# FNet mixing plus MLP on one core: the work around the paired blocks in another order

## The chip, the cores and the metric

The kernel runs on one NeuronCore of a Trainium2 chip. The metric is the device time of one execution, in microseconds (us). Three executions of the kernel before took 879.98, 880.30 and 880.65 us.

## The reference

The input x has 2048 rows and 640 columns. After a layer norm it goes through two branches, whose results are added to x. All inputs and the output are float32.

```python
xn = (x - mean) / sqrt(var + 1e-5)                       # over the 640 columns
a, b = xn @ wr.T, xn @ wi.T                              # DFT along the columns, wr and wi 640 x 640
A = cr @ a - ci @ b                                      # DFT along the rows, real part, cr and ci 2048 x 2048
B = gelu(xn @ w1 + b1) @ w2 + b2                         # w1 640 x 1536, w2 1536 x 640
out = x + A + B
```

## The kernel before

Every operand of a matmul is split in two, a high half that ScalarE rounds to fp32r (`high`, line 182) and a low half that VectorE gets by subtraction (`low`, line 185); `product` (lines 303 to 305) then takes three matmuls: high x high, high x low, low x high. Each reads 128 x 128 weights against 512 columns. The order of all instructions is written out by hand: every engine runs its own list in the order in which the code issues it, and waits where its data or its place is not ready. A tile of a pool with one buffer can be written only when every reader of the tile that lay there before is done, stores to memory included. Loads and stores go through the queue of SyncE (SP), in that same order: a load or store that waits holds up all behind it.

The 2048 rows are four row blocks t = 0 to 3 of 512, and the 1536 hidden units are 12 chunks of 128. The kernel runs in these stages:

- **Block 0, a loop over i = 0 to 9.** Step i splits W1 of chunk i + 3 (`prep_w1`) and W2 of chunk i + 1 (`prep_w2`), issues two weight loads, calls `background(i)`, and then does `hidden(i + 2)` (15 matmuls, line 321), its gelu and split (the tile `hs`), and `output(i)` (15 matmuls). `background` normalizes the rows of blocks 2 and 1 (`ln_stats`, `ln_scale`, `ln_apply`), stores them to the DRAM buffer xs, and loads them back, turned, as Z["b"] (block 2, tile z_b) and Z["a"] (block 1, tile row). `make_forms` turns parts of Z with VectorE and splits them; each is a *form* (ua, va, oa from "a"; vb, ob, t1 from "b"; t2, t3, t4 from sums and differences of both).
- **Six paired blocks, k = 0 to 5.** `pair(k)` does the first MLP layer of blocks 1 and 2 for two hidden chunks at once, by a scheme in which 7 products take the place of 8 (Strassen's, in Winograd's form). `window` multiplies a *piece* of the weights (A, B, C, D, each split in a high half "h" and a low half "l" by `make_pieces`, with "+" for the sums between) with a form. The gelu of block 1 stays on chip (a1, a2), that of block 2 goes to the DRAM buffer gs (`keep`). `put_out` places output matmuls of block 1 between the windows. `beside_pair(k, at)` holds other work, and is called in a block in the order at = 2, 5, 6, 3, 7, 4: finishing block 0 (`finish`: ScalarE adds the bias, VectorE turns the block, GpSimd adds it to x in xo[0]), storing it (`store_sums`), copying rows in DRAM (`by_chunks`), and splitting the seven forms of the column DFT matrices wr and wi (`prep_w`, `put_w`), which are stored to the buffers wits.
- **A loop over p = 0 to 13.** Step p does `output` of block 2 from the stored units, or, at the end, block 3's first hidden chunks. `between(p)` holds the rest: finishing block 1, layer norm of the last rows (x12 to x15), Z["z"] for block 3, splitting W1 again, loading xo[2].
- **Block 3, and from 290 us on the DFT along the rows**, in which TensorE's work is matmul after matmul.

In `put_w` before, five of the forms share three places of the tile wst in turn, and two lie in the pool rows under the tag "yt":

```python
        if w in (3, 4):
            t = rows.tile([P, 2, 2 * P], F32R, tag="yt", bufs=2, name=f"wst{w}_{j}")
        else:
            t = A["wst"][:, A["puts"] % 3]
```

Names that the prediction uses: "Al" is the low half of piece A; C2 is the window (z_, "C", 2, "vb") of a block, t4 the window (x_, b, 0, "t4"); zc is ScalarE's copy of the bank z_ that must be made before C2 overwrites it; b2 is the second unit of block 2 in a paired block. The tiles wst, xo[0], z_b and others lie in turn in the one place of the pool outp (`zo_tile`).

Of the kernel before, what the change touches and what calls it, by code (L numbers as in the profile page):

```python
# [15 lines left out]
P = 128  # L16
# [9 lines left out]
def kernel(  # L26
# [198 lines left out]
    def ln_apply(c, eng=nc.vector):  # L225
        m = MV[:, slot[c]]
        eng.tensor_scalar(xt[c], xt[c], m[:, 0:1], m[:, 3:4], op0=ALU.subtract, op1=ALU.mult)
        nc.sync.dma_start(xs[c * P : (c + 1) * P], xt[c])
# [146 lines left out]
    def add_block(dst, e, acc, name, eng=nc.gpsimd, bias=None, home=rows):  # L375

        if bias is not None:
            nc.scalar.activation(acc, acc, AF.Identity, bias=bias)
        yt = home.tile([P, TB], F32, tag="yt", bufs=2, name=name)
        nc.vector.transpose(yt, acc)  # L380
        d = dst[:, :, e * B : (e + 1) * B]
        eng.tensor_tensor(d, d, yt.rearrange("p (n i) -> p n i", i=B), op=ALU.add)  # L382
# [21 lines left out]
    stores = []  # L404

    def put_away():
        for f in stores:
            f()
        stores.clear()

    def put_w(w, j, main, odd=None, negative=False):

        n = GWIDE[w] * P
        if w in (3, 4):
            t = rows.tile([P, 2, 2 * P], F32R, tag="yt", bufs=2, name=f"wst{w}_{j}")
        else:
            t = A["wst"][:, A["puts"] % 3]
            A["puts"] += 1
        split(t[:, 0, : 2 * P], t[:, 1, : 2 * P], main)
        if odd is not None and not negative:  # L420
            split(t[:, 0, 2 * P :], t[:, 1, 2 * P :], odd)
        elif odd is not None:
            h, l = t[:, 0, 2 * P :], t[:, 1, 2 * P :]
            nc.scalar.activation(h, odd, AF.Copy, scale=-1.0)
            nc.vector.scalar_tensor_tensor(l, odd, -1.0, h.bitcast(F32), op0=ALU.mult, op1=ALU.subtract)
        stores.append(lambda: nc.sync.dma_start(wits[w][j], t[:, :, :n].bitcast(F32)))

    def prep_w(j, k):
# [20 lines left out]
        put_away()  # L449
# [252 lines left out]
    def background(i):  # L702

        if i == 0:
            ln_apply(0)
            ln_apply(1)
            A["rows_b"] = zo_tile("rows_b", (P, NC, D))
            for c in range(2 * NC, 3 * NC):
                load_x(c, home=A["rows_b"])
        if i == 1:  # L710
            ln_apply(2)
            ln_apply(3)
            for c in range(NC, 2 * NC):
                load_x(c)
        if i == 2:
            for c in range(2 * NC, 3 * NC):
                ln_stats(c)
        if i == 3:
# [3 lines left out]
            ln_stats(4)  # L722
            ln_stats(5)
            Z["b"] = zo_tile("z_b")
            load_z(Z["b"], 2)
        if i == 4:
            ln_stats(6)
            ln_stats(7)
# [4 lines left out]
            load_z(Z["a"], 1)  # L733
        if i == 6:
            new_forms()
            make_forms("b", "vb0", "vb1", "ob0")
        if i == 7:
            make_forms("a", "ua0", "ua1", "va0", "va1", "oa0")
        if i >= 8:
            (ua, va), (ub, vb) = ((Z[k][:, :, : 2 * B], Z[k][:, :, 2 * B : 4 * B]) for k in "ab")  # L740
        if i == 8:
            add(ub, ub, ua, ALU.subtract)
            make_forms("b", "t10", "t11")
            add(vb, vb, ub, ALU.subtract)
        if i == 9:
            add(ua, vb, ua, ALU.subtract)
            add(va, va, vb, ALU.subtract)
            turn_x("t20", "b")
            turn_x("t21", "b")
# [6 lines left out]
    def new_forms():  # L756
        spare = []
        for k, name in enumerate(("ua", "va", "t1", "vb")):
# [4 lines left out]
        XF["oa0"], XF["ob0"] = spare[:2], spare[2:]  # L763
# [73 lines left out]
    def finish(t, *es):  # L837
        for e in es:
            add_block(xo[t], e, oacc[t][e], f"ot{t}_{e}", bias=b2c[:, e : e + 1])
# [5 lines left out]
    def store_sums(t):  # L845
        for k, (c0, c1) in enumerate(YCOLS):
            nc.sync.dma_start(ys[k][t], xo[t][:, :, c0:c1])  # L847

    LASTK = NF // 2 - 1

    def beside_pair(k, at):

        if k == 0:
# [6 lines left out]
            if at == 7:  # L860
                finish(0, 0, 1, 2)
            if at == 4:
                finish(0, 3, 4)
            return
        j = k - 1
        if at == 2 and k > 1:
            prep_w(j - 1, 2)
        if at == 5:
            if k > 1:
                put_away()  # L870
            else:
                store_sums(0)
            if k < NT:
                by_chunks(k - 1)
        if at == 6:
            turn_w(0, j)
            turn_w(1, j)
        if at == 3:
            if k == 1:
                A["wst"], A["puts"] = zo_tile("wst", (P, 3, 2, 3 * P), F32R), 0  # L880
# [4 lines left out]
            put_away()  # L885
# [3 lines left out]
        if at == 7:  # L889
# [6 lines left out]
            put_away()  # L896
# [3 lines left out]
        if k == LASTK and at == 4:  # L900
# [703 lines left out]
```

## Time and profile before

| | us |
|---|---|
| three runs | 879.98, 880.30, 880.65 (median 880.3) |
| profiled execution | 878.27 |
| its span, first to last instruction | 876.3 |
| TensorE (PE) busy | 852.8 |
| VectorE (DVE) busy | 683.4 |
| ScalarE (ACT) busy | 364.8 |
| GpSimd (POOL) busy | 22.1 |
| mean DMA rate over the span | 201 GB/s |

In the profile's lines a time is us from the span's start. A line of a timeline gives start, length, engine, line of the kernel, operation, tiles (out<-in), shapes and count, and in brackets the idle time of the engine before it and what ended that. "SPq" is SyncE's queue at the moment of issue. A line of the waits gives who waited for whom: us in total, how often, the longest. A line of the windows gives a stretch, its length, and each engine's busy time and instructions in it, then the clock granted to TensorE, the busy share of the DMA engines, and GB/s.

### The profile page before, as it was taken

What the parts mean: (1) busy time and instruction counts of PE and PEld (TensorE: products, weight loads), DVE (VectorE), ACT (ScalarE), POOL (GpSimd) and SP (SyncE); (2) the same over time, 40 slices, a digit from 0 to 9 for tenths busy, and PEclk for the clock granted to TensorE, in tenths of its full rate; (3) what the DMA queues carried; (4) which work ended last, traced back from release to release, by engine and by line L of the source; (5) the groups of instructions that cost most, each with busy time, mean ns of one, the idle gap of its engine ahead of it and who ended that gap; (6) DMA issues with size and microseconds to landing.
All of it is one profiled execution on the core that took longest, in us unless ns stands there. A gap on an engine that the chain in (4) does not pass through costs nothing.

```text
span 876.3 us, 10521 instructions
## 1 busy us (share of the span) xinstructions
PE 852.8 (97%) x3718; PEld 700.2 (80%) x3718; DVE 683.4 (78%) x892; ACT 364.8 (42%) x520; POOL 22.1 (3%) x22
## 2 busy tenths in 40 slices
PE   8999889999989999999999999999999999999996
PEld 6888667788867888888888888888888888888885
DVE  6787887675773478988988798898977898885586
ACT  5564456455534356543433434332322423223241
POOL 0000030000111100000000000000000000000000
PEclk9999899999999999999999999999999999999999
DMA  6987488879987993968583459855575779804464
GB/s 182 301 239 165 94 200 270 261 225 302 277 229 158 223 422 159 215 143 196 155 216 85 99 145 321 232 104 154 142 179 190 235 192 229 317 18 174 120 186 84
DMA packets 227187, 171.76 MB, mean 196 GB/s; under 512 B 83648, under 2 KB 197056, under 8 KB 226496
## 3 DMA queue, kind: packets, MB, share of 16 engines
q1 hardware_dynamic: 221184, 169.13, 70.5%
q10 hardware_dynamic: 5952, 1.97, 0.9%
q8 instruction: 29, 0.48, 0.2%
q14 instruction: 22, 0.18, 0.1%
HBM read 124.92 MB, written 51.38 MB: 201 GB/s over the span
## 4 chain that ended last, share of the span: by engine, by line
PE 67%; DMA 4%; SPq 2%; DVE 1%; POOL 1%; issue 0%; ACT 0%; POOLq 0%; DVEq 0%; ACTq 0%
PE banks L303 21%; PE banks L304 21%; PE banks L305 21%; PE banks L321 3%; DMA xab<-in_A_x_dram 1%; DMA w1r<-in_B_w_dram 1%; DMA xo<-in_A_x_dram 1%; SPq L281 1%; DMA wit<-wst 1%; POOL xo L382 0%; SPq L847 0%; SPq L373 0%; DMA xs<-row 0%; SPq L258 0%; DVE as L185 0%
## 5 line engine op out<-in xcount | busy, mean ns | idle before, releaser
L304 PE MATMUL banks<-as,xab 128*128 128x512 f32 x407 | 158.4, 389 | 0.0
L303 PE MATMUL banks<-as,xab 128*128 128x512 f32 x407 | 158.4, 389 | 0.0
L305 PE MATMUL banks<-as,xab 128*128 128x512 f32 x407 | 158.4, 389 | 0.0
L182 ACT ACTIVATE as<-r 128x1024 fp32r<-128x1024 f32 x80 | 85.0, 1062 | 173.6 <-PE banks L305 148.8
L185 DVE TENSOR_TENSOR as<-r,as 128x1024 fp32r<-128x1024 f32 x80 | 97.2, 1216 | 39.1 <-ACT as L182 39.1
L304 PEld LDWEIGHTS banks<-as,xab 128*128 128x128 f32 x407 | 76.4, 188 | 16.2 <-DVE as L185 0.4
L305 PEld LDWEIGHTS banks<-as,xab 128*128 128x128 f32 x407 | 76.4, 188 | 15.9
L303 PEld LDWEIGHTS banks<-as,xab 128*128 128x128 f32 x407 | 76.4, 188 | 15.9
L303 PE MATMUL banks<-as,xc 128*128 128x512 f32 x224 | 87.1, 389 | 0.0
L304 PE MATMUL banks<-as,xc 128*128 128x512 f32 x224 | 87.1, 389 | 0.0
L305 PE MATMUL banks<-as,xc 128*128 128x512 f32 x224 | 87.1, 389 | 0.0
L182 ACT ACTIVATE as<-rt 128x1024 fp32r<-128x1024 f32 x32 | 34.0, 1063 | 69.8 <-PE banks L305 57.9
L321 PE MATMUL banks<-xt,xab 128*128 128x512 f32 x240 | 56.8, 390 | 0.3 <-ACT xt L182 0.3
L185 DVE TENSOR_TENSOR hs<-ab,hs 128x512 fp32r<-128x512 f32 x36 | 26.7, 743 | 36.2 <-ACT hs L182 36.2
L321 PEld LDWEIGHTS banks<-xt,xab 128*128 128x128 f32 x240 | 44.7, 188 | 10.3 <-ACT xt L182 1.3
L305 PEld LDWEIGHTS banks<-as,xc 128*128 128x128 f32 x224 | 42.0, 188 | 8.8
L303 PE MATMUL banks<-hs,xc 128*128 128x512 f32 x120 | 47.0, 392 | 2.1 <-DVE ot L380 2.1
L303 PEld LDWEIGHTS banks<-as,xc 128*128 128x128 f32 x224 | 42.0, 188 | 8.7
L304 PEld LDWEIGHTS banks<-as,xc 128*128 128x128 f32 x224 | 42.0, 188 | 8.7
L305 PE MATMUL banks<-hs,xc 128*128 128x512 f32 x120 | 46.7, 389 | 0.0
L304 PE MATMUL banks<-hs,xc 128*128 128x512 f32 x120 | 46.7, 389 | 0.0
L185 DVE TENSOR_TENSOR as<-rt,as 128x1024 fp32r<-128x1024 f32 x32 | 38.8, 1212 | 5.3 <-ACT as L182 5.3
(200 smaller groups left out, 1601.7 us busy)
## 6 DMA issues: line engine op xcount, KB each, us to landing
raw<-in_A_dft_seq_re_dram SPq DMA_DIRECT2D x64, 256.0 KB, 5.3
raw<-in_A_dft_seq_im_dram SPq DMA_DIRECT2D x64, 256.0 KB, 4.9
w1r<-in_B_w_dram SPq DMA_DIRECT2D x136, 80.0 KB, 2.7
wit<-wst SPq DMA_DIRECT2D x20, 384.0 KB, 3.1
ws<-wit SPq DMA_DIRECT2D x15, 384.0 KB, 5.5
xn<-xs SPq DMA_DIRECT2D x4, 1280.0 KB, 7.8
forms_ab<-xab SPq DMA_DIRECT2D x4, 1280.0 KB, 8.1
xab<-wit SPq DMA_DIRECT2D x13, 384.0 KB, 4.4
```

The source lines that it names most:

```text
L182: nc.scalar.activation(h, s, AF.Copy)
L185: nc.vector.tensor_tensor(l, s, h.bitcast(F32), op=ALU.subtract)
L281: eng.dma_start(t[q * B : (q + 1) * B], v[q, :, :, f0 : f0 + P])
L303: nc.tensor.matmul(acc, wh, mh, start=first, stop=False, skip_group_check=goes_on)
L304: nc.tensor.matmul(acc, wh, ml, start=False, stop=False, skip_group_check=goes_on)
L305: nc.tensor.matmul(acc, wl, mh, start=False, stop=last, skip_group_check=goes_on)
L321: nc.tensor.matmul(acc, W1[i][:, a, j * P : (j + 1) * P], XT[j][:, b], start=n == 0, stop=n == len(steps) - 1)
```

## The change

It moves work among the steps above, and puts some tiles elsewhere; the arithmetic stays.

- **background**: all four `ln_apply` of block 0's rows in step 0, their stores behind the loads of the next rows (`put_rows`); the statistics of blocks 2 and 1 one step sooner; the forms from "b" in step 5, from "a" in steps 6 and 7; the sums and differences one step sooner, the turns of t2 ahead of those of step 9.
- **new_forms**: the forms lie in the four places in another order, and the fourth place is opened a step later.
- **make_pieces** in steps of another order (D ahead of C, the B piece of block 0 after the loop); in block k = 0 the pieces D and C for the next block come after the gelu of a2.
- **finish of block 0**: blocks 0 and 1 after the gelu of a2 in k = 0 (`at == 4`), block 2 at `at == 2` and blocks 3 and 4 at `at == 5` of k = 1; some turned blocks lie in the pool mr under the tag "zt".
- **put_out**: 3 and 3 output groups where there were 2 and 4.
- **put_w**: a place of its own for each form, form 2 in two parts (one store more); the last three forms at the end of their own block (`at == 4`) and not in the next.
- **LASTK (k = 5) and between**: load_unit(6, 7) ahead of x14 and x15; statistics of the last rows in p = 0 to 2, `ln_apply` in p = 2; the turns of Z["z"] in p = 7 to 9; load_xo(2) in p = 9; finish of blocks 1 and 2 spread over other steps and places.

```diff
-    def ln_apply(c, eng=nc.vector):
+    def ln_apply(c, eng=nc.vector, put=True):
         m = MV[:, slot[c]]
         eng.tensor_scalar(xt[c], xt[c], m[:, 0:1], m[:, 3:4], op0=ALU.subtract, op1=ALU.mult)
+        if put:
+            put_rows(c)
+    def put_rows(c):
         nc.sync.dma_start(xs[c * P : (c + 1) * P], xt[c])
...
-    def add_block(dst, e, acc, name, eng=nc.gpsimd, bias=None, home=rows):
+    def add_block(dst, e, acc, name, eng=nc.gpsimd, bias=None, home=rows, tag="yt"):
...
             nc.scalar.activation(acc, acc, AF.Identity, bias=bias)
-        yt = home.tile([P, TB], F32, tag="yt", bufs=2, name=name)
+        yt = home.tile([P, TB], F32, tag=tag, bufs=2, name=name)
         nc.vector.transpose(yt, acc)
...
-    stores = []
-    def put_away():
-        for f in stores:
-            f()
-        stores.clear()
     def put_w(w, j, main, odd=None, negative=False):
...
         n = GWIDE[w] * P
-        if w in (3, 4):
-            t = rows.tile([P, 2, 2 * P], F32R, tag="yt", bufs=2, name=f"wst{w}_{j}")
+        st, last = A["wst"], j == ND - 1
+        if w in (0, 1, 6):
+            k = w % 5 if w < 6 else 2
+            t = st[:, k * 6 * P : (k + 1) * 6 * P].rearrange("p (a b) -> p a b", a=2)
+            parts = [(t, 0, n)]
         else:
-            t = A["wst"][:, A["puts"] % 3]
-            A["puts"] += 1
+            name = f"wst{w}_{j}"
+            if w in (2, 3):
+                t = rows.tile([P, 2, 2 * P], F32R, tag="yt", bufs=2, name=name)
+            elif not last:
+                t = early.tile([P, 2, 2 * P], F32R, tag="w2r", bufs=3, name=name)
+            elif w == 4:
+                t = mr.tile([P, 2, 2 * P], F32R, tag="zt", bufs=2, name=name)
+            else:
+                t = st[:, : 4 * P].rearrange("p (a b) -> p a b", a=2)
+            parts = [(t, 0, 2 * P)]
+            if w == 2:
+                parts.append((st[:, 18 * P : 20 * P].rearrange("p (a b) -> p a b", a=2), 2 * P, n))
+        to = parts[-1][0][:, :, -P:]
         split(t[:, 0, : 2 * P], t[:, 1, : 2 * P], main)
         if odd is not None and not negative:
-            split(t[:, 0, 2 * P :], t[:, 1, 2 * P :], odd)
+            split(to[:, 0], to[:, 1], odd)
         elif odd is not None:
-            h, l = t[:, 0, 2 * P :], t[:, 1, 2 * P :]
+            h, l = to[:, 0], to[:, 1]
             nc.scalar.activation(h, odd, AF.Copy, scale=-1.0)
             nc.vector.scalar_tensor_tensor(l, odd, -1.0, h.bitcast(F32), op0=ALU.mult, op1=ALU.subtract)
-        stores.append(lambda: nc.sync.dma_start(wits[w][j], t[:, :, :n].bitcast(F32)))
+        for t, c0, c1 in parts:
+            nc.sync.dma_start(wits[w][j][:, :, c0:c1], t.bitcast(F32))
...
             put_w(5, j, r2)
-        put_away()
...
         if i == 0:
-            ln_apply(0)
-            ln_apply(1)
+            for c in range(NC):
+                ln_apply(c, put=False)
             A["rows_b"] = zo_tile("rows_b", (P, NC, D))
...
                 load_x(c, home=A["rows_b"])
+            for c in range(NC):
+                put_rows(c)
         if i == 1:
-            ln_apply(2)
-            ln_apply(3)
+            ln_stats(8)
+            ln_stats(9)
             for c in range(NC, 2 * NC):
...
         if i == 2:
-            for c in range(2 * NC, 3 * NC):
-                ln_stats(c)
-        if i == 3:
+            ln_stats(10)
+            ln_stats(11)
             ln_scale(NC)
...
                 ln_apply(c)
-            ln_stats(4)
-            ln_stats(5)
             Z["b"] = zo_tile("z_b")
             load_z(Z["b"], 2)
+        if i == 3:
+            for c in range(NC, 2 * NC):
+                ln_stats(c)
         if i == 4:
-            ln_stats(6)
-            ln_stats(7)
             ln_scale(NC)
...
             load_z(Z["a"], 1)
+        if i == 5:
+            new_forms(0, "vb", "ua", "va")
+            make_forms("b", "vb0", "vb1", "ob0")
         if i == 6:
-            new_forms()
-            make_forms("b", "vb0", "vb1", "ob0")
+            new_forms(3, "t1")
+            make_forms("a", "ua0", "ua1", "oa0")
         if i == 7:
-            make_forms("a", "ua0", "ua1", "va0", "va1", "oa0")
-        if i >= 8:
+            make_forms("a", "va0", "va1")
+        if i >= 7:
             (ua, va), (ub, vb) = ((Z[k][:, :, : 2 * B], Z[k][:, :, 2 * B : 4 * B]) for k in "ab")
+        if i == 7:
+            add(ub, ub, ua, ALU.subtract)
         if i == 8:
-            add(ub, ub, ua, ALU.subtract)
             make_forms("b", "t10", "t11")
...
         if i == 9:
+            turn_x("t20", "b")
+            turn_x("t21", "b")
             add(ua, vb, ua, ALU.subtract)
             add(va, va, vb, ALU.subtract)
-            turn_x("t20", "b")
-            turn_x("t21", "b")
             load_xo(0)
...
-    def new_forms():
-        spare = []
-        for k, name in enumerate(("ua", "va", "t1", "vb")):
+    spare = []
+    def new_forms(k0, *names):
+        for k, name in enumerate(names, k0):
             f = place(f"xab{k}", (P, 5, TB))
...
             spare.append(f[:, 4])
-        XF["oa0"], XF["ob0"] = spare[:2], spare[2:]
+        XF["ob0"], XF["oa0"] = spare[:2], spare[2:]
...
-    def finish(t, *es):
+    def finish(t, *es, home=None):
         for e in es:
-            add_block(xo[t], e, oacc[t][e], f"ot{t}_{e}", bias=b2c[:, e : e + 1])
+            add_block(xo[t], e, oacc[t][e], f"ot{t}_{e}", bias=b2c[:, e : e + 1], **(home or {}))
...
             nc.sync.dma_start(ys[k][t], xo[t][:, :, c0:c1])
+    in_zt = {"home": mr, "tag": "zt"}
...
                 load_w(1, 0)
-            if at == 7:
-                finish(0, 0, 1, 2)
             if at == 4:
-                finish(0, 3, 4)
+                finish(0, 0, 1)
             return
         j = k - 1
-        if at == 2 and k > 1:
-            prep_w(j - 1, 2)
-        if at == 5:
-            if k > 1:
-                put_away()
-            else:
+        if k == 1:
+            if at == 2:
+                finish(0, 2, home=in_zt)
+            if at == 5:
+                finish(0, 3, home=in_zt)
+                finish(0, 4)
+            if at == 6:
                 store_sums(0)
+        if at == 6:
             if k < NT:
                 by_chunks(k - 1)
-        if at == 6:
             turn_w(0, j)
...
             if k == 1:
-                A["wst"], A["puts"] = zo_tile("wst", (P, 3, 2, 3 * P), F32R), 0
+                A["wst"] = zo_tile("wst", (P, NB * DQ), F32R)
             prep_w(j, 0)
...
                 load_w(1, j + 1)
-            put_away()
             if k == LASTK:
...
                 prep_w(j, 2)
-            put_away()
+        if k < LASTK and at == 4:
+            prep_w(j, 2)
         if k == LASTK and at == 2:
...
         if k == LASTK and at == 4:
+            for i in range(6, 8):
+                load_unit(i)
             load_x(14)
             load_x(15)
-            for i in range(6, 8):
-                load_unit(i)
             load_xo(1, place("xab2", (P, NB, DQ), F32))
...
         beside_pair(k, 6)
-        put_out(2 if k else 0)
+        put_out(3 if k else 0)
         window(z_, "C", 2, "vb", False, ("C", 4, "ob0"))
...
         beside_pair(k, 3)
-        put_out(4 if k else 0)
+        put_out(3 if k else 0)
         window(x_, "D", 0, "t3", False)
...
         keep(b2_, unit(b2_, x_, zc))
-        make_pieces(k + 1, *(("Dl",) if k else ("Bh", "Bl", "+", "Dh", "Ch", "Dl", "Cl")))
+        make_pieces(k + 1, *(("Dl",) if k else ("Bh", "Bl", "+")))
         beside_pair(k, 7)
...
         gelu(a2, x_)
+        if not k:
+            make_pieces(1, "Dh", "Dl", "Ch", "Cl")
         beside_pair(k, 4)
...
-        if p == 1:
-            finish(1, 3, 4)
-        if p == 2:
+        if p == 0:
             ln_stats(12)
             ln_stats(13)
-        if p == 3:
+        if p == 1:
+            finish(1, 3, 4, home=in_zt)
             ln_stats(14)
+        if p == 2:
             ln_stats(15)
...
             new_xt(3)
+        if 4 <= p < 7:
+            finish(1, p - 4)
         if p == 5:
-            finish(1, 0, 1)
             by_chunks(3)
-        if p == 6:
-            finish(1, 2)
-        if p == 7:
-            transpose_z("x30", Z["z"], 0)
-        if 7 <= p < 7 + ND:
-            j = p - 7
+        for j in {7: (0,), 8: (1, 2), 9: (3, 4)}.get(p, ()):
+            if j == 0:
+                transpose_z("x30", Z["z"], 0)
             if j + 1 < ND:
...
             prep_xt(f"x3{j}", j)
+        if p == 9:
+            load_xo(2)
         if p == 10:
...
             open_place(*PLACES[2])
-            load_xo(2)
         for n in {0: (0,), 4: (1,), 5: (2,), 6: (3,), 7: (4,), 8: (5,), 9: (6,), 10: (7,), 11: (8,), 12: (9, 10), 13: (11,)}.get(p, ()):
...
             new_pieces()
-            make_pieces(0, "Ah", "Bh", "Al", "Bl")
+            make_pieces(0, "Ah", "Al")
             more_forms()
...
         output(i)
-    make_pieces(0, "+", "Ch", "Dh", "Cl", "Dl")
+    make_pieces(0, "Bh", "Bl", "+", "Dh", "Dl", "Ch", "Cl")
     split_x("t20")
...
             gelu(g + 2, acc, fill)
-            finish(2, 1, 2)
+            finish(2, 1, 2, home=in_zt)
             store_sums(2)
...
```

## The prediction

> **What bounds the kernel now.** I read the page first, then the windows, the waits of TensorE, and the timelines around each of its gaps.
>
> ```profile
> PE 852.8 (97%) x3718; PEld 700.2 (80%) x3718; DVE 683.4 (78%) x892; ACT 364.8 (42%) x520; POOL 22.1 (3%) x22
> ...
> PEclk9999899999999999999999999999999999999999
> ```
>
> TensorE is busy for 852.8 of 876.3 us, and its clock dips in two slices. The windows say where the rest lies (columns: length, PE, PEld, DVE, ACT, POOL, clock, DMA share, GB/s):
>
> ```profile
> 20.00:70.00 50.00, 50.00 (x222) 41.40 (x222) 37.38 (x77) 28.12 (x41) 0.00 (x0) 1.00 0.90 261
> ...
> 88.30:98.40 10.10, 5.96 (x16) 4.40 (x16) 9.20 (x16) 3.79 (x8) 0.00 (x0) 0.66 0.56 115
> ...
> 290.00:860.00 570.00, 569.92 (x2515) 471.62 (x2514) 470.68 (x487) 214.92 (x253) 0.00 (x0) 1.00 0.68 185
> ```
>
> After 290 TensorE never waits, so what is won or lost before 290 arrives at the end unchanged. Its waits (total, times, longest):
>
> ```profile
> PE banks L305 <- DVE w1f L185: 4.1, 1, 4.1
> PE banks L303 <- ACT zc L182: 3.7, 3, 1.8
> PE banks L303 <- ACT hs L182: 2.7, 1, 2.7
> PE banks L303 <- DVE ot L380: 2.1, 3, 1.1
> ...
> PE banks L303 <- ACT ab L340: 0.9, 1, 0.9
> ```
>
> Matmuls start every 0.227 us where nothing waits. Measuring each gap against that pitch, slow starts at half clock included, gives the us lost: **A** 88.6 to 98.3, 6.8 (stall 4.3, half clock 2.5); **B** 117.4 and 123.6, 3.1; **D** 144.4 and 164.2, 4.4; **E** 251 to 259, 5.3; **F** 281 to 286, 2.9. Together 22.5 us, all that this change can win. The timelines say what stands behind them (landings of single transfers, used below, are the trace's for each DMA issue):
>
> ```profile
> 72.88 1.30 DVE L262 STREAM_TRANSPOSE ztua<-row 128x512 f32<-128x512 f32 x2 [4.54 <-DMA row<-xs]
> ...
> 93.09 0.79 PE L305 MATMUL banks<-xab,w1f 128*128 128x512 f32 x1 [4.14 <-DVE w1f L185]
> ...
> 120.51 4.70 SPq L847 DMA_DIRECT2D ys<-xo  x3
> ...
> 121.69 1.16 ACT L182 ACTIVATE w1f<-w1r 128x384 fp32r<-128x384 f32 x2 [0.74 <-DMA w1r<-in_B_w_dram]
> ...
> 157.76 0.62 ACT L182 ACTIVATE wst<-row 128x256 fp32r<-128x256 f32 x2 [4.07 <-DMA wit<-wst]
> ...
> 166.41 0.71 PE L303 MATMUL banks<-xab,w1f 128*128 128x512 f32 x1 [1.83 <-ACT zc L182]
> ...
> 251.44 1.30 DVE L262 STREAM_TRANSPOSE ztx<-z 128x512 f32<-128x512 f32 x2 [4.70 <-DMA z<-xs]
> ...
> 280.81 7.25 POOL L382 TENSOR_TENSOR xo<-xo,ot 128x512 f32<-128x512 f32 x5 [34.60 <-DMA xo<-in_A_x_dram]
> ```
>
> **A, the layer norm and the forms.** Before, VectorE idles until Z["a"] lands (72.70) and then works without a break to the low half "Al" that TensorE needs: 72.88 to 92.25, 19.4 us. So A hangs on that landing. The change moves the statistics a step ahead, but load_z for Z["a"] stays in background(4), behind the same transfers, and from 20 to 70 the DMA engines are 0.90 busy. What comes free is small. The four stores of the second rows went out behind w1r and w2r loads that took 2.6 us to land (45.16 to 47.74); those now land behind Z["b"], where such a pair takes 1.9 (59.45 to 61.33): 0.7 sooner. The x loads no longer wait for the late stores of background(1): at most 1.1 more. I take 71.2, within 70.5 to 72.7. Against that, the forms from "a" move from i = 7 to i = 6, ahead of the low halves of hs, W1 and W2 that ran before the landing: 2.1 us (66.15 to 68.25) now stand behind it. Al starts at 71.4 + 19.4 + 2.1 = 92.9, and TensorE resumes 0.8 later, at 93.7, where it was 93.1. Part of the stall moves forward: W1 of hidden(10) is split only at 71.4 + 6.15 = 77.6 (the form steps of 61.37 to 67.50), and TensorE wants it at 75.1, a new stall of 2.4. Then 2.4 remain at Al. Loss in A: 4.9 without half clock, **1.9 won**.
>
> [...] By the rows, the stall of 4.14 cost 2.5 more at half clock, that of 2.67 at 254 cost 2.4, that of 1.83 at 166.41 cost 1.7, and those of 0.92 and 1.44 at 118.7 and 125.5 nothing: near 2 us either may follow. [...] I take none after Al, because a half clock after the first of the two stalls would be used up in the second.
>
> **B, gelu ahead of the bias.** The gelu no longer stands behind three bias steps (117.39 vanishes, 1.4), and put_out(3) instead of 2 gives 0.7 of cover. But the next block's "Bh" waits for a w1r load (row 121.69), which is now issued after gelu, hs, Dh and Dl: from the end of t4, 0.2 + 0.7 + 0.6 + 0.6 + 0.7 = 2.8 to its issue and 5.3 to land (116.20 to 121.53): 8.1. t4 ends 18.6 after TensorE resumes (82 matmuls at 0.227), at 112.3, so the load lands at 120.4. Behind it stand Bh and Ah 1.3, now bias 0.57 and the turn of block 2 0.65, then add 0.65, gelu 0.75, hs 0.6, zc 0.65: 5.2. C2 starts at 125.6. Unhindered it would be 93.7 + 121 x 0.2267 = 121.1. Loss 4.5 against 3.1: **1.4 lost**; bounds 0.7 won (bias and turn hidden) to 3 lost.
>
> **C, a place for each form.** New: wst lies in the one place of the pool "outp", where xo[0] lay, and its first writing waits for store_sums(0). Before, those stores land at 128.83, ahead of the first form at 131.06. Now blocks 3 and 4 are turned at `at == 5`, behind "+": counted from the w1r landing, add 3.25, Al, Bl, hs 2.1, "+" 2.0, port sharing with POOL 0.6 (row 241.95: 1.77 for a low half of 0.69), two turns 1.3, the last POOL add 1.9: about 11, and the store 3.6 to 4.1: the place opens at 15.0. ScalarE waits there, with Dh, and VectorE's low halves and the add of b2 queue behind; t4 overwrites the bank that this add reads. 15.0 + 2.5 = 17.5 after the landing is 137.9. TensorE is ready at 125.6 + 36 x 0.2267 = 133.8. **4.1 lost**, a wait that is not in the trace of before; bounds 0 (stores hidden) and 6.6 (with 2.5 of half clock). I take 4.1: C2 starts after 4.3 us with three matmuls in them, so the half clock falls there, inside this slack.
>
> **D, the later blocks.** With own places nothing waits for a store's landing (4.07 at 157.76 and its smaller kin), the last three forms fill ScalarE's idle 1.17 before L329, and put_out(3) adds 0.7 of cover. zc is then ready about 8.4 after t4 starts, C2 wants it at 10.9. **4.4 won**; at least 3, as the blocks shrink to 84 x 0.2267 = 19.0 us with the same bytes (DMA share up to 0.91 already). One more store per block, 0.45 on SP, lies in its 4 to 5 us of idle time.
>
> **E, last rows.** SP issues the stores of x12 to x15 at 237.46 only as slots come free, while ln_apply was done at 234.3, and the DMA share from 204 to 240 is 1.02. Doing ln_apply a step sooner changes nothing: the z load lands at 251.3 relative to the blocks. load_unit(6, 7) now stands ahead of x14 and x15, so x15 lands some 3 us later (231.9, where unit 7 landed), and the apply holds VectorE into step 5: a stall of 2.5 there, taken off the one at step 10. Half clock then overlaps the wait for z. **0.9 won**; bounds 2.4 won, 1 lost.
>
> **F, x sooner.** load_xo(2) leaves in step 9 behind the last turn of z3 (about 259.5) and not at 271.66, lands near 268, and POOL starts when the first block is turned at 277.8. With two places in "yt" and two in "zt" the turns wait once, 0.3. **2.6 won**; if it were late again, 0.
>
> **Sum.** -1.9 + 1.4 + 4.1 - 4.4 - 0.9 - 2.6 = -4.3. The profiled execution took 878.27 (span 876.3 and 2.0 around it), so 874.0; the median of the runs is 880.3, and I predict 876.0.
>
> **Rivals.** *Slower:* half clock follows the short stalls. After Al it costs 2.4, which passes through t4 to the w1r landing and the rest; after the stall in C another 2.4; after the one in E, where it then delays step 10, 2.4: -4.3 + 7.2 = +2.9, 883.2. With two of the three the sum is +0.5, no change; the third decides. For it: 1.83 idle at 166.41 sufficed. Against: 1.44 did not. *Faster:* the landings come sooner. The DMA share in 50 to 52.5 is 0.19 and in 62.5 to 65 is 0.48; if these 3.3 us fill, A and all behind it shrink by 3.3 (872.7), and if also the stores in C are hidden it is 868.6; I take 870.5. Against: SP waits for stores before each z load, then as now. *It does not do what it says:* the landing stays at 72.7 and E gives nothing: -4.3 + 1.5 + 0.9 = -1.9, and with C 1 us dearer -0.9, 879.4.
>
> **How the numbers follow.** Forecast 0.45 (own range 873 to 878.4), faster rival 0.22, no change 0.10, slower rival 0.23. A measurement of this kernel tells 0.2% (1.8 us) from no change; so faster 0.67, same 0.10, slower 0.23. Half of each outer rival is left outside the range: 868.5 to 883.
>
> **What would show it.** Right: a PE wait of about 2 us at L321 near 75; a shorter one at Al near 93; ACT waiting near 135 to write wst, with `DMA ys<-xo` named, and PE behind it; no waits on zc after 140; z landing about 41 us after the last block's first gs store; no wait on ot near 281. Wrong: Z["a"] landing before 69, or wst written without a wait.

## The result, and the profile after

The change makes the kernel slower: 887.47, 888.06 and 888.08 us, median 888.06 against 880.3, a ratio of 1.0086 with a 95% interval of 1.0063 to 1.0109. The forecast was 876.0 (868.5 to 883). The profiled execution took 888.06, span 886.0; that of before took 878.27. The two profiles thus differ by 9.8 us, the medians by 7.8; the stretches below are reckoned between the profiles.

The page: TensorE works 3.4 us more than before for the same 3718 matmuls, which ran slower, and the dip in the clock now lies in the fourth slice (66 to 89 us).

```profile
PE 856.2 (97%) x3718; PEld 701.0 (79%) x3718; DVE 684.9 (77%) x892; ACT 364.4 (41%) x520; POOL 22.8 (3%) x22
...
PEclk9998999999999999999999999999999999999999
```

The windows (length, PE, PEld, DVE, ACT, POOL, clock, DMA share, GB/s). The stretch after 290 still runs nearly without waits. In 117 to 137 all engines are less than two thirds busy except TensorE, and the DMA engines have a share of 0.30: a chain of single steps, each waiting for the last.

```profile
117.00:137.00 20.00, 13.93 (x46) 9.96 (x45) 12.88 (x21) 10.75 (x18) 6.35 (x5) 0.83 0.30 71
...
290.00:860.00 570.00, 568.27 (x2502) 468.97 (x2501) 469.13 (x487) 215.57 (x257) 7.29 (x5) 1.00 0.68 185
```

TensorE's waits (us, times, longest). The wait on "DVE w1f" (Al) is gone, and of the three on zc one is left (1.5); the first three lines here are new or larger.

```profile
PE banks L307 <- DVE ot L384: 6.5, 4, 3.4
PE banks L325 <- ACT as L182: 3.9, 1, 3.9
PE banks L308 <- DVE hs L185: 2.4, 3, 1.3
PE banks L307 <- ACT hs L182: 2.3, 1, 2.3
...
PE banks L307 <- DVE ab L463: 1.3, 1, 1.3
```

The timeline of after, at the places that answer to those shown of before. Lines have moved by 4 to 11: product is 307 to 309, hidden 325, the gelu 344, the turns of z 266 and of the sums 384.

```profile
58.59 2.38 SPq L232 DMA_DIRECT2D xs<-row  x4
...
73.39 1.30 DVE L266 STREAM_TRANSPOSE ztua<-row 128x512 f32<-128x512 f32 x2 [9.08 <-DMA row<-xs]
...
78.81 6.59 PE L325 MATMUL banks<-xt,as 128*128 128x512 f32 x15 [3.94 <-ACT as L182]
...
117.24 0.69 ACT L344 ACTIVATE ab<-banks,b1c 128x512 f32<-128x512 f32 x1 [4.03 <-DMA gs<-ab]
...
125.49 1.15 ACT L182 ACTIVATE w1f<-w1r 128x384 fp32r<-128x384 f32 x2 [4.12 <-DMA w1r<-in_B_w_dram]
...
127.99 0.50 PE L307 MATMUL banks<-hs,xc 128*128 128x512 f32 x1 [3.38 <-DVE ot L384]
...
130.47 0.79 PE L307 MATMUL banks<-xab,w1f 128*128 128x512 f32 x1 [1.51 <-ACT zc L182]
...
140.49 1.12 ACT L182 ACTIVATE wst<-row 128x256 fp32r<-128x256 f32 x4 [3.52 <-DMA ys<-xo]
...
187.20 0.69 ACT L344 ACTIVATE ab<-banks,b1c 128x512 f32<-128x512 f32 x1 [5.13 <-DMA gs<-ab]
...
233.40 0.72 DVE L384 STREAM_TRANSPOSE ot<-banks 128x512 f32<-128x512 f32 x1 [2.73 <-DMA wit<-wst]
...
261.37 1.30 DVE L266 STREAM_TRANSPOSE ztx<-z 128x512 f32<-128x512 f32 x2 [6.17 <-DMA z<-xs]
...
288.46 0.74 ACT L182 ACTIVATE xab<-w1r 128x640 fp32r<-128x640 f32 x1 [6.28 <-DMA w1r<-in_B_w_dram]
```

Us lost in each stretch, reckoned as in the prediction (gaps against the pitch of 0.227 us, half clock included):

| stretch | before | forecast | after |
|---|---|---|---|
| A, layer norm and forms | 6.8 | 4.9 | 7.1 (4.1 at hidden(10), 3.0 half clock) |
| B, 117 to 136 | 3.1 | 4.5 | 9.8 (1.7 D, 3.5 turn, 1.8 zc, 2.8 half clock) |
| C, wait for wst | 0 | 4.1 | 1.6 |
| D, later blocks | 4.4 | 0 | 1.4 (at 186) |
| E, last rows and z | 5.3 | 4.4 | 9.4 (4.5 at 232 to 245, 4.9 at z) |
| F, xo[2] | 2.9 | 0.3 | 2.8 |
| sum | 22.5 | 18.2 | 32.1 |

### The profile page after: what moved, and what is told of

Same layout as the page of the kernel before. It is cut to its first block, busy times and chain, and to the rows that moved or that the text cites. A ratio compares the mean times of both kernels' runs of the same rounds, so it can differ in the third digit from the quotient of the medians.

```text
span 886.0 us, 10517 instructions
## 1 busy us (share of the span) xinstructions
PE 856.2 (97%) x3718; PEld 701.0 (79%) x3718; DVE 684.9 (77%) x892; ACT 364.4 (41%) x520; POOL 22.8 (3%) x22
## 4 chain that ended last, share of the span: by engine, by line
PE 74%; DMA 12%; DVE 6%; SPq 3%; ACT 2%; issue 1%; POOL 1%; DVEq 0%; ACTq 0%; POOLq 0%
PE banks L308 23%; PE banks L307 23%; PE banks L309 23%; PE banks L325 5%; DMA gs<-ab 2%; DMA w1r<-in_B_w_dram 1%; DMA xs<-row 1%; DMA row<-in_A_x_dram 1%; DMA wit<-wst 1%; DVE hs L185 1%; DMA xn<-xs 1%; SPq L285 1%; PE banks L662 1%; SPq L398 1%; DMA ys<-xo 1%
## 5 line engine op out<-in xcount | busy, mean ns | idle before, releaser
L307 PE MATMUL banks<-hs,xc 128*128 128x512 f32 x120 | 47.9, 399 | 6.8 <-DVE ot L384 6.5
L308 PE MATMUL banks<-hs,xc 128*128 128x512 f32 x120 | 47.3, 394 | 2.0 <-DVE hs L185 2.0
L309 PE MATMUL banks<-hs,xc 128*128 128x512 f32 x120 | 47.0, 391 | 0.0
```

Source lines behind the costliest of these rows:

```text
L307: nc.tensor.matmul(acc, wh, mh, start=first, stop=False, skip_group_check=goes_on)
L308: nc.tensor.matmul(acc, wh, ml, start=False, stop=False, skip_group_check=goes_on)
L309: nc.tensor.matmul(acc, wl, mh, start=False, stop=last, skip_group_check=goes_on)
```

## The experiments

All are timed against the kernel before on the same chip; "us" are medians. On those chips the kernel before took 878.7 to 881.4. What is lost in a stretch is read from one profiled execution of each kernel.

### Each part alone

The change falls into four parts that can be put into the kernel before one at a time.

```diff
# oA: background, new_forms, the order of the pieces of block 0
# oB: in k = 0 and 1
+        gelu(a2, x_)
+        if not k:
+            make_pieces(1, "Dh", "Dl", "Ch", "Cl")
+            finish(0, 0, 1)             # and 2, 3, 4 in k = 1, store_sums(0) at 6; put_out 3 and 3
# oW: put_w with places of its own, stores at once
+        if k < LASTK and at == 4:
+            prep_w(j, 2)                # by_chunks(k - 1) at 6
# oE: load_unit(6, 7) ahead of x14, x15; between() of the change; finish(2, 1, 2) in zt
```

> The kernel before with part A of the change alone (background, the order of the forms, the order of the pieces of block 0). Theory: the landing of Z["a"] decides, it stays near 73, and W1 of hidden(10), now split behind the forms from "a", makes TensorE wait there (4.1 and 3.0 of half clock, 74 to 85) in place of the stall at Al (4.3 and 2.5): between 0 and +0.6 us, and no change in later stretches. Rival (the prediction's step): landing near 71, two short stalls, no half clock, 1.9 us faster.

> The kernel before with part B alone (gelu of a2 ahead of pieces and bias in k = 0, finish of block 0 spread over two blocks, output groups 3 and 3). Theory: this gelu writes an ab place that is free only when the gs store of b2 has landed (117.2 in the trace of after); pieces, w1r load, bias and turn now queue behind that wait, so the loss at 117 to 136 grows from 3.1 to 9.8, and the later store_sums(0) makes the first write of wst wait (1.6 more): +7 to +8.5 us, nearly all of the whole change's loss. Rival: the loss there came from the shift in A, and B alone gives the predicted +1.4, or +5.5 with the wait for wst at its predicted 4.1.

> The kernel before with the places of the wr and wi forms alone (part W: a place for each form, stores at once, the last three forms at the end of their block, the row copy at 6). Theory: the zc stalls of k = 2 and 3 go (4.4), a stall of about 1.3 comes at the gelu of a2 in k = 3, where the row copy lies ahead of the gs store; no wait for wst, as store_sums(0) is early: -2.5 to -3.5 us. Rival: the wait for the one place of outp comes with the new wst (the prediction's step C, +4.1), so -0.3.

> The kernel before with the end alone (load_unit(6, 7) ahead of x14 and x15, last rows sooner, turns of z in three steps, load_xo(2) in step 9). Theory: x15 lands some 7 us later, its statistics and the apply hold VectorE ahead of the low halves of hs: 2.4 us of new stalls near 230 to 236; the stall of 1.8 at the turn of block 4 needs the change's wst place under zt too and does not come here; z lands no sooner (0.3), the stall near 281 stays (w1r loads behind the x load): +2 us. Rival: all of the 4.1 us that the whole change lost from 232 on comes from this part alone: +4. Second rival (the prediction): -3.5.

> The changed kernel itself once more, beside the next three on the same chip: about +7 us against the kernel before (it was +7.8). The parts alone gave -1.2 (A), +5.0 (B), -2.3 (W), 0 (E) by their ratios, together +1.5. Theory: the rest is in two meetings of parts, the turn of block 4 that waits for a form's store under zt (E with W, 1.8), and z: TensorE no longer waits longer for it in E alone because z lands by the DMA traffic and not by the blocks, so what the stalls of 232 to 245 cost is on top. Rival: chip to chip noise, then +1.5 here.

| run | us | before | ratio (95%) |
|---|---|---|---|
| A alone | 879.53 | 879.78 | 0.9986 (0.9971 to 1.0001) |
| B alone | 886.07 | 879.78 | 1.0057 (1.0034 to 1.0080) |
| W alone | 877.55 | 879.78 | 0.9974 (0.9953 to 0.9995) |
| E alone | 880.25 | 879.78 | 0.9999 (0.9982 to 1.0016) |
| whole change | 886.64 | 880.51 | 1.0065 (1.0049 to 1.0081) |

B alone costs most of what the whole costs (5.0 us by its ratio, 3.0 to 7.0, and not the theory's 7 to 8.5), and its profile shows the same chain: 9.4 lost from 118 to 136 and 2.4 at the wait for wst. W alone wins 2.2: the zc stalls go (0.9 is left, at the gelu of a2 near 180), and nothing waits for wst, since the sums of block 0 are stored early there; part comes back at z, where its profiled execution lost 8.4 and the one of before 5.3. E alone costs 2.2 at 232 to 238 and saves 2.6 at z: no change, so neither the theory's +2 nor the rivals' +4 and -3.5. A alone loses 8.0 in its stretch with Z["a"] at 74.5; the three kernels timed beside it that lack A (oB, oW, oE) lost 7.6, 8.9 and 7.8 there with Z["a"] at 76.0, 75.0 and 74.7: A alone changes nothing that is clear of noise. The four ratios add up to +0.16%, the whole is +0.65%; with the intervals, 4 us, give or take 4, come from parts meeting. One such meeting is seen (the turn at 233.40 waits for a form's store, which needs E's turn and W's place under zt); the rest was not traced.

### B: what holds up the next pieces

```diff
# mORD, from the changed kernel
+        if not k:
+            make_pieces(1, "Dh", "Dl", "Ch", "Cl")
         gelu(a2, x_)
-        if not k:
-            make_pieces(1, "Dh", "Dl", "Ch", "Cl")
# mZT, from the changed kernel
-        gelu(a2, x_)
+        if k < LASTK:
+            zg = mr.tile([P, TB], F32, tag="zt", bufs=2, name=f"zg{k}")
+            split_unit(a2, unit(a2, x_, a=zg))
# mORD2, from mORD
-                finish(0, 0, 1)
+                finish(0, 0, 1, 2)
-            if at == 2:
-                finish(0, 2, home=in_zt)
```

> The changed kernel, but in k = 0 the pieces Dh, Dl, Ch, Cl go before the gelu of a2 again; the finish steps stay where the change put them. Theory (the gelu stands in line for the gs store, 4.0 us, and holds up the pieces and the w1r load): Dh near 115, the load lands near 122 and not 125.3, no stall at D, the stalls of 117 to 136 fall from 9.8 to 4 to 6, the wait for wst grows by at most 1.5: 3 to 5 us faster than the changed kernel. Rival (the bias, turns and adds of blocks 2 to 4, now in k = 1, are the cost): at most 1 us faster.

> The changed kernel in its own order, but the gelu of a2 in k = 0 to 4 writes a tile of zt, so that it needs no place of ab. Theory: ScalarE's waits for gs stores (4.0 at 113 to 117, 3.2 at 163, 5.1 at 182) go, the gelu runs near 115, the w1r load lands 2.3 sooner, the stall at D (1.7) and the one at 186 (1.4) go: 3 to 5 us faster than the changed kernel. Rival (as for the run before): only the 1.4 at 186.

> As the run with the pieces ahead of the gelu of a2, and block 2 of the sums finished in k = 0 too, as before the change. Theory (the turn of block 2 stood behind the w1r landing, and the output of block 1 that takes its bank waits for it): the stall of 1.45 near 123 goes, that for zc (1.8) stays: 117 to 136 lose 3 to 4 (before 3.1, the run without this 5.3), 1 to 2 us faster than that run. Rival (the stall only moves into the one for zc): 5 lost, no change.

mORD took 881.85, 4.8 less than the changed kernel beside it (1.0028, 1.0013 to 1.0044, against before). The timeline of its ScalarE: the piece Dh now runs at 114.96 while the gelu's place is still taken, the gelu waits only 0.84, and the w1r load lands at 122.3 and not 125.3.

```profile
114.96 0.63 ACT L182 ACTIVATE w1f<-w1r 128x512 fp32r<-128x512 f32 x1 [1.60 <-DVE w1r L463]
...
117.60 0.69 ACT L344 ACTIVATE ab<-banks,b1c 128x512 f32<-128x512 f32 x1 [0.84 <-DMA gs<-ab]
```

117 to 136 lose 5.3 instead of 9.8. mZT keeps the change's order and takes the wait away: gelu at 114.1, landing at 122.5, no stall at D, none at 186. It takes 883.8, 2.8 less than the changed kernel: 117 to 136 still lose 6.9 (the turn of block 2 and zc stay, with half clock behind them), and the stalls of 228 to 237 cost 5.6, where run aft lost 5.3. The rival of both, that bias and turns in k = 1 are the cost, holds only for the rest: mORD2 loses 3.2 there (before 3.1) and takes 880.3 against 878.7 (1.0015, 1.0002 to 1.0028, which overlaps the interval of mORD). With B out of the way, C comes in full:

```profile
135.69 1.12 ACT L182 ACTIVATE wst<-row 128x256 fp32r<-128x256 f32 x4 [3.50 <-DMA ys<-xo]
...
138.16 0.50 PE L307 MATMUL banks<-as,w1f 128*128 128x512 f32 x1 [2.86 <-DVE ab L463]
```

3.1 at that wait and 1.6 of half clock behind it, 4.7 in all; in the changed kernel it was 1.6 because TensorE came late itself.

### A: what sets the landing of Z["a"]

```diff
# mNP, from the changed kernel
-            for c in range(NC):
-                put_rows(c)
+            nc.sync.dma_start(xs[:TB], x[:TB])        # in step 9
# a2, from the changed kernel: all of step 4 moves into step 3
-        if i == 4:
             ln_scale(NC)
```

> The changed kernel without the four stores of the normalized rows of block 0 in step 0; instead the raw rows are copied in memory after step 9, so the first 512 rows go unnormalized into the column DFT. 1.3 MB less are moved before Z["a"]. Theory (the landing of Z["a"] decides A, and the DMA traffic decides the landing): at some 260 GB/s that is 5 us, Z["a"] lands 3 to 5 sooner, the 7.1 of A fall to 3 or less; 3 to 5 us faster than the changed kernel. Rival (VectorE's own work between the landing and Al, or the statistics, decide): landing the same within 1, A the same within 1.

> The changed kernel with scale, apply, stores and the load of Z["a"] one step sooner still (step 3 instead of 4). In its trace the apply was done at 51.5, but the stores went out only at 58.2, behind the w1r and w2r loads of step 4, which filled SP's slots. Theory (the place in SP's queue decides the landing): stores out near 54, Z["a"] lands 4 to 6 us sooner (67 to 69), the 6.7 to 7.1 of A fall to 2 or less; 4 to 6 us faster than the changed kernel. Rival (the DMA engines' own traffic decides, as the 1.6 us of the run without 1.3 MB may say): the landing moves by less than 2, and w1r of a later chunk is late instead: within 2 us of the changed kernel.

mNP: 1.3 MB less, and Z["a"] lands 1.6 sooner (71.4 against 73.0), A loses 5.0 and not 6.7; 885.2 us, 1.4 less (1.0054, 1.0041 to 1.0067, which overlaps the interval of the changed kernel). The theory's 3 to 5 us are not there: traffic is one part only. a2 tells the other. The timeline of a2, SP's queue, VectorE and TensorE:

```profile
53.83 3.81 SPq L232 DMA_DIRECT2D xs<-row  x4
...
70.12 1.30 DVE L266 STREAM_TRANSPOSE ztua<-row 128x512 f32<-128x512 f32 x2 [6.24 <-DMA row<-xs]
...
92.26 0.80 PE L309 MATMUL banks<-xab,w1f 128*128 128x512 f32 x1 [1.94 <-DVE w1f L185]
92.86 0.63 PE L307 MATMUL banks<-xab,w1f 128*128 128x512 f32 x1
```

The stores leave at 53.8, not 58.6, and Z["a"] lands at 70.0, 3 sooner. But A still loses 5.2 (1.3 near 75, 2.1 at Al, 1.7 half clock), and the time is 882.66 against 878.9 (1.0049, 1.0032 to 1.0066): an interval that meets that of the changed kernel. VectorE now works from 70.1 to the end of Al at 92.2, 22.1 us, where before it was 19.4: what the landing gives, the longer list ahead of Al takes. Both theories had half of it.

### E: what sets the wait for z

```diff
# mE, from the changed kernel: x14, x15 ahead of load_unit(6, 7) again, and
-            finish(1, 3, 4, home=in_zt)
+            finish(1, 3, home=in_zt)
+            finish(1, 4)
# c1, from the kernel before
             load_z(Z["z"], 3)
+            load_xo(1, xo[1])           # was ahead of the last rows; blocks 3, 4 added here
-            finish(1, 0, 1)             # and finish(1, 2): now in steps 8 to 10, in zt
# c4, from c1: load_xo(1) at the end of step 5, behind its w1r load; by_chunks(3) in step 9
```

> The changed kernel with x14 and x15 ahead of units 6 and 7 again, and block 4 of the sums turned into yt and not zt (where it waits for a form's store). Theory (z lands by the DMA traffic, not by the blocks): the stalls of 232 to 245 (4.5 to 5.1) fall to 1 or less, but TensorE then waits longer for z, near 7 to 8 with half clock in place of 4.2 to 4.9: 1 to 2.5 us faster than the changed kernel. Rival: each stall counts in full, 4 to 5 us faster.

> The kernel before, with one thing else: the load of xo[1] (1.3 MB) goes out behind the loads of z and not ahead of the last rows; blocks 3 and 4 of the sums are turned into zt and added later, blocks 0 to 2 in steps 8 to 10, the turns of z lie in yt. Theory (traffic ahead of z sets its landing): z lands at 245 to 247 and not at 251.3, the 5.3 of E fall to 1 or less: 3 to 5 us faster than before. Rival (the statistics and the apply set it): z lands within 1.5 of 251, same time as before.

> As the run with xo[1] behind z, but the load of xo[1] behind the w1r loads of steps 4 and 5 too, and the row copy of 1.3 MB in step 9 and not 5. Theory (there the wait of 253.4 named w1r, so the w1r load, not z, came last): z lands near 246 and this w1r near 248, the 5.3 that the kernel before loses at 251 to 259 fall to 1.5 or less: 3 to 4 us faster than the kernel before. Rival (VectorE's and ScalarE's work on z, sums and W1 between 246 and 262 is the limit): 4 or more still lost, same time as before.

mE: 884.6 against 878.9 (1.0073, 1.0058 to 1.0088), no gain on the changed kernel. The stall at the turn is gone. Of those behind x15 2.5 stay: it lands at 236.5 now, and step 2 still wants it sooner. At z 7.1 are lost where it was 4.2. The rival (each stall counts in full) falls. In these four traces the stores of the last rows leave SP when the last quarter of xo[1] has landed, whatever VectorE did: 237.39 and 237.46 before, 245.96 and 246.02 after, 238.57 and 238.63 in oE, 245.28 and 245.34 in mE; z lands 13.9 to 15.3 behind that. The order in SP's queue goes with it: the last quarter of xo[1] stands eight places ahead of the first of these stores, and none of the 648 loads and stores of the trace of before, nor of the 653 of after, that have one eight places ahead left before that one had landed, while 92 and 116 left before the one seven places ahead had (in all twenty traces none and 2,270 of 13,027).

c1 breaks this link: the stores leave at 233.3, z lands at 246.8, 4.5 sooner than before. But now the next in the queue is late (SP and ScalarE of c1):

```profile
233.28 1.89 SPq L232 DMA_DIRECT2D xs<-row  x4
237.94 2.54 SPq L262 DMA_DIRECT2D z<-xs  x4
240.52 4.44 SPq L378 DMA_DIRECT2D xab<-in_A_x_dram  x4
...
253.43 0.74 ACT L182 ACTIVATE as<-w1r 128x640 fp32r<-128x640 f32 x1 [5.25 <-DMA w1r<-in_B_w_dram]
```

7.4 lost, 881.16 against 878.9 (1.0028, 1.0011 to 1.0045). c4 puts w1r ahead of the x load; then the turn of a sum waits for GpSimd, which waits for x:

```profile
257.21 0.72 DVE L385 STREAM_TRANSPOSE ot<-banks 128x512 f32<-128x512 f32 x1 [6.79 <-POOL xab L395]
```

8.6 lost there and 9.1 between 284 and 297, where the row copy now stands ahead of xo[2] (in c6 below that copy alone comes with 8.2 lost there); 887.77 against 878.7 (1.0097, 1.0082 to 1.0112). c4's theory falls: z, w1r and x are each due within some 10 us, and in the three orders that were run the one put last stopped TensorE: z before (5.3 lost), w1r in c1 (7.4), x in c4 (8.6).

### F: xo[2] against w1r

```diff
# mF, from the changed kernel: load_xo(2) behind the w1r load of step 11
-        if p == 9:
+        if p == 11:
             load_xo(2)
```

> The changed kernel with the load of xo[2] two steps later, behind the w1r loads of steps 9 to 11 and the store of the sums of block 1. Theory (at 288.5 ScalarE waited 6.3 us for a w1r load that stood behind the x load and the sums' store, and bias and turns stood behind it): that wait falls below 3, xo[2] lands just in time, the 2.8 lost at 290 fall to 1 or less: 1.5 to 2.5 us faster than the changed kernel. Rival (the turns wait for places and GpSimd whatever the loads): still 2.5 to 3 lost, no change.

888.17 against 878.7 (1.0109, 1.0092 to 1.0126). ScalarE's wait of 6.3 at 288.5 is gone, as expected. But the x load now waits behind eight w1r loads (5.74 us to issue), lands at 292.2, and the turns wait for GpSimd: 5.4 lost instead of 2.8.

```profile
278.22 5.74 SPq L285 DMA_DIRECT2D w1r<-in_B_w_dram  x8
284.00 2.03 SPq L377 DMA_DIRECT2D xo<-in_A_x_dram  x4
...
292.54 7.22 POOL L386 TENSOR_TENSOR xo<-xo,ot 128x512 f32<-128x512 f32 x5 [37.07 <-issue]
```

### A version that beats both

c7 is the kernel before with part W (the last w4 in the wst tile), part A, and Z["a"] stored and loaded in step 3; B and E stay as before. c3 is c7 with xo[1] as in c1; c5 is c3 with the loads of c4, W1 of chunk 10 split ahead of the forms, and load_xo(2) in step 10; c6 is c7 with the row copy in step 9.

```diff
# c7, from the kernel before with parts W and A
-                t = mr.tile([P, 2, 2 * P], F32R, tag="zt", bufs=2, name=name)
+                t = st[:, 6 * P : 10 * P].rearrange("p (a b) -> p a b", a=2)
-        if i == 4:                      # scale, apply, load_z(Z["a"], 1) in step 3
```

> What the runs point to, put together from the kernel before: the change's order of the forms with Z["a"] stored and loaded in step 3, the change's places for the wr and wi forms (the last w4 in the wst tile, not in zt), xo[1] behind z; the blocks' gelu and finish stay as before. Theory: 4 to 6 from A, 3 from the later blocks, 3 to 5 from z: 867 to 871. Rival: what is won early is lost again at z and at xo[2] (about 281): 874 to 877.

> The combined kernel again, with the order of loads of c4, W1 of chunk 10 split ahead of the forms from "a", and the load of xo[2] in step 10. Theory: from the combined kernel's 875.5 another 2 at A, 5 to 6 at 244 to 256 and up to 2 at 277 go: 866 to 869. Rival: the stall at A only moves to Al and the loads at the end push each other: 873 to 876.

> The combined kernel with xo[1] where the kernel before loads it, and the row copy of block 3 (1.3 MB) in step 9 and not 5. Theory (the stretch is bound by its traffic, and the copy stands among z, w1r and x there): the loss at z falls below 5, 3 us faster than the next run: 870 to 873. Rival (z is ahead of the copy in the queue and lands no sooner): the same as the next run within 1.

> The combined kernel with xo[1] where the kernel before loads it, the row copy in step 5 as before. Theory: what A and the later blocks win (4 and 4) comes back in part at z, whose landing does not move with the blocks: 8 lost there, 874 to 876, as the combined kernel. Rival: z moves with the blocks, 5 lost there, 871 to 873.

| run | us | before | ratio (95%) |
|---|---|---|---|
| c3 | 875.52 | 878.9 | 0.9963 (0.9950 to 0.9976) |
| c5 | 882.56 | 878.7 | 1.0037 (1.0022 to 1.0052) |
| c6 | 877.64 | 881.36 | 0.9958 (0.9935 to 0.9981) |
| c7 | 875.24 | 881.36 | 0.9935 (0.9912 to 0.9959) |

c7 has the lowest ratio of all the runs, though its interval overlaps that of c3. It loses 4.5 at A (Z["a"] at 70.7), 3.2 at B, nothing from 124 to 243, 5.9 at z and 4.8 at xo[2]. z landed 6.3 sooner than before, with the blocks: by its mechanism c7's rival was nearer, though the time of 875.24 lies in the theory's range. c3's rival held. In c5 the rival's two mechanisms came, the stall moved to Al (9.6 lost in A) and at 253 and 280 the loads pushed each other (7.4 and 8.1), but they cost more than its 873 to 876. c6 met neither its theory nor its rival (2.4 more than c7). It lost 7.5 at z, so the copy was not what delayed it; in step 9 it holds up the store of the sums and the load of xo[2] instead (8.2 lost there). Its profiled execution, at 881.6, was the longest of its twelve.

## Why the prediction was wrong, step by step

**A** (forecast 1.9 won, 0.3 lost). The stall at hidden(10) was named, and its chain held: W1 was ready 5.4 after VectorE began on Z["a"] (forecast 6.15). Two terms failed. The landing: 73.2, not 71.2, because the stores of x4 to x7 stood behind the w1r and w2r loads of step 4, which took 4.4 us to issue, and left at 58.6, later than before (56.4). Three of those loads left only as quarters of Z["b"], eight places ahead, landed (54.05, 55.64, 57.21). And half clock, taken as none, came after that stall of 3.9 and cost 3.0. Al then did not wait, since TensorE was late already.

**B** (1.4 lost, 6.7 lost). From the landing of w1r to C2 the forecast of 5.2 was right to 0.1 (125.3 to 130.47), and so was the load's own time (5.3 forecast, 119.94 to 125.33). The step that failed is the issue of that load: the sum from the end of t4 began with "0.2" to the gelu, and it took 2.6 (114.65 to 117.24). The gelu writes an ab place whose reader, the gs store of b1, lands at 117.13 (the expectation of oB names b2, whose store lands at 117.75). Before, three bias steps stood in that gap, that store had landed at 114.89, and the gelu ran without a wait:

```profile
117.96 0.69 ACT L340 ACTIVATE ab<-banks,b1c 128x512 f32<-128x512 f32 x1
```

"The gelu no longer stands behind three bias steps" priced them at 1.4 and won nothing. The stall also came in three pieces, 1.7 at D, 3.5 at the turn of block 2 and 1.8 at C2, with half clock of 2.8 behind the last; the prediction had it at C2 alone.

**C** (4.1 lost, 1.6 lost). Mechanism and times were right: first write of wst 15.0 behind the landing (140.3 forecast from it, 140.49 measured), t4 at 17.5 (142.8, 142.96). The loss was smaller because B made TensorE late; with most of B out of the way (mORD2) it was 4.7. The 0.6 for GpSimd in that sum names a cause that no run shows. What the traces of before and after show are lengths: the ten low halves of hs that overlap a GpSimd add took 1.10 to 1.79 us, the other 86 at most 0.69.

**D** (4.4 won, 3.0 won). The zc stalls went. The 1.4 at 186 is the gelu of a2 again, behind a gs store that the row copy, now issued ahead of it, delayed to 187.1; it goes in mZT.

**E** (0.9 won, 4.1 lost). The stall of 2.5 behind x15 came as forecast; "taken off the one at step 10" holds in oE (2.2 for 2.6), not in the whole, where z landed 15.3 and not 14.6 behind xo[1] and 2.4 of half clock followed. The stall of 1.9 at the turn of block 4, whose place under zt held a form's store, was not foreseen.

**F** (2.6 won, 0.1 won). The x load left in step 9 as forecast, at 270.0 in this later stretch, and had landed at 279.7, 10 us ahead of the first turn. But the w1r loads behind it came late, and ScalarE waited 6.3 us for one, with the bias ahead of that turn behind it. This was not in the sum: the earlier load was priced for itself and not for what it pushed back.

The misses: A 2.2, B 5.3, C -2.5, D 1.4, E 5.0, F 2.5, together 13.9. The rival on the slower side had the sign and not the cause: it put half clock after Al, C and E, and it came after hidden(10), B and z. The upper end of the prediction's own range, 878.4, lies one half clock of 2.4 above 876.0, which no run bears out: the changed kernel had three (6.83 us from 78.22, 6.83 from 129.42, 3.41 from 265.96), none of them at C. Neither sign that the prediction gave for being wrong came (Z["a"] landed at 73.2, and wst was written after a wait of 3.52): both watched A and C, and the largest miss was in B.

## What to carry to other kernels

Before an instruction is moved ahead in an engine's list, ask what it waits for there: here a gelu whose place was still being stored waited 4.03 us and held up all that it was moved past. A load that is issued sooner is not free: name the load it now precedes and when that one is due (with xo[2] ahead of it, a w1r load made ScalarE wait 6.28 us), and look up what stands eight places ahead of it: in these traces no load or store of SP left before that one had landed. Where several transfers fall due together, price the last of them and not the one that the trace names (5.3 us lost with z last, 7.4 with w1r, 8.6 with x), and check a stretch by taking out one part at a time: here one part of four, by itself, cost most of it.

## What the runs showed of the hardware

In these traces the length of a gap alone did not tell whether half clock followed. TensorE idled 1.94 before 92.26 in a2 (lines above), and the matmuls behind it take 0.63 and not 0.39 each. In the second run of the changed kernel it idled 2.41, and the next matmuls are back at 0.40 and 0.39:

```profile
234.79 0.50 PE L307 MATMUL banks<-hs,xc 128*128 128x512 f32 x1 [2.41 <-DVE ot L384]
```

The two differ in where the gap lies. In all twenty traces the recorded clock changes only on a grid of points 3.41 us apart, whose position against the span differs from run to run: half clock is first recorded from 91.44 us in before and from 78.22 in after, 13.22 apart, which is no multiple of 3.41. Between 20 and 860 us, half clock lasts one or two steps of the grid each time (6.83, 3.41 and 3.41 us in before; 6.83, 6.83 and 3.41 in after). It was granted after every step at full clock in which TensorE had idled 1.88 us or more in all, after none with 1.67 or less, and after 7 of the 15 steps between. In before it followed steps with 2.49, 1.83 and 2.59 idle and none with 1.44 or less; in after steps with 3.34, 2.46 and 1.84 and none with 1.64 or less. The gap in a2 lies whole in one step, and the clock in the next is 0.50; that in aft is cut into 1.69 and 0.72 (busy 1.72 and 2.69 of 3.41), and the clock stays at 1.00 (two windows of a2, then one of aft):

```profile
88.88:92.29 3.41, 1.47 (x8) 0.89 (x6) 3.41 (x5) 0.08 (x1) 0.00 (x0) 1.00 0.01 2
92.29:95.70 3.41, 3.41 (x8) 2.73 (x9) 3.27 (x8) 0.98 (x2) 0.00 (x0) 0.50 0.98 209
...
234.07:237.48 3.41, 2.69 (x12) 2.24 (x13) 0.66 (x1) 0.00 (x0) 0.00 (x0) 1.00 1.08 285
```

An estimate from the 1.88 and 3.41 us above: a gap of 3.8 us or more puts at least 1.9 into one step, wherever the grid lies, and half clock would follow it; the 3.94 at hidden(10) put 3.34 into one step, and it did. For a gap of 1.9 to 3.7 us the estimate gives no answer without the position of the grid, and that was not the same in before and after.
